# The order of the numerator's and the denominator's steps within a unit of a rational feed-forward

## The chip, the cores and the metric

One core of one Trainium2 chip runs the whole program. The core has five engines that matter here, each with its own queue of instructions executed in order: TensorE (PE, matrix products, with its weight loads listed as PEld), VectorE (DVE), ScalarE (ACT), GpSimd (POOL) and SyncE (SP), which issues most of the transfers. The metric is the device time of one execution in microseconds (us); the figure to be predicted is the median of the runs of the changed kernel.

## What is computed

Two stages follow each other. The first is a delta rule over 768 time steps for 4 batches of 8 heads, head size 48:

```python
for t in range(S):
    kt, vt, bt = (k_n[:, :, t], v[:, :, t], beta[:, :, t, None])
    y[:, :, t] = np.einsum('bhd,bhde->bhe', q[:, :, t], state)
    v_old = np.einsum('bhde,bhd->bhe', state, kt)
    state = state + bt[:, :, :, None] * np.einsum('bhd,bhe->bhde', kt, vt - v_old)
```

Its output, as 3072 tokens of 384 numbers, is the input x of the second, in which a rational function stands between two matrix products (384 to 2048 and back):

```python
h = x @ w_in
P = a[0] + a[1] * h + a[2] * h2 + a[3] * h3
Q = 1.0 + np.abs(b[0]) * np.abs(h) + np.abs(b[1]) * h2
g = P / (Q + 1e-06)
return (g @ w_out).astype(np.float32)
```

Here h2 and h3 are the square and the cube of h. The inputs and the output are 32-bit floating point, but for the two weight matrices, which arrive in 64 bit.

## The kernel before

The sequence is cut into 12 chunks of 64 steps. For each chunk an attention part (lines 489 to 722, all engines) makes the 256 tokens of the chunk, two batches on the 128 partitions and two pairs of them side by side; the state passes from chunk to chunk. `tokens` (L726 on) transposes and scales the tokens, `scalars` makes the coefficients of the rational function for the chunk. Before all this the weights are converted from 64 bit and kept in SBUF as pairs of 16-bit numbers, each product of two such pairs being three passes on PE.

The rational stage runs in units. A unit n is one chunk and one eighth of the 2048 hidden features: 256 features in two groups of 128 on the partitions, by 256 tokens, so each tile is 128 x 512. There are 96 units, and each has four steps:

- `hidden(n)`: 18 products on PE into the PSUM tile ph (two of these exist, so ph of unit n + 2 takes the place of ph of unit n).
- `numerator(n)`, the function that the change touches. ACT reads ph twice: L823 makes u = A3·h + a2 and L825 makes z = |B1·h|. DVE then reads ph three times: L826 u ← h·u, L828 w ← (z + B0)·h, L830 u ← (u + A1)·h. Between these ACT takes the absolute value of w in place (L829). u, w and z are SBUF tiles of three buffers each (tags mu, mw, mr). In some units POOL adds A0 at the end (L834).
- `quotient(n)`: ACT takes the logarithm of w + Q0 (L841) and the exponential of its negative (L842), which gives r, the reciprocal of the denominator, in the tile of z. DVE makes the upper half of g (L847, or L845 in units where POOL has added A0), then what this half has left over (L848, and L852 or POOL's L850), and POOL the lower half (L853).
- `accumulate(n)`: 12 products on PE of g with w_out into the output's accumulators, read out by ACT at L882 after the last unit of a chunk.

The program's loop interleaves them, with the attention of later chunks in between:

```python
for n in range(N + 2):
    if n < N:
        numerator(n)
    if 0 <= n - 1 < N:
        quotient(n - 1)
    attention(*divmod(n + SHIFT, NU))
    if 0 <= n - 2 < N:
        accumulate(n - 2)
    if n + 1 < N:
        hidden(n + 1)
```

This order isn't yet that of the engines' queues. The kernel is built under a planner (L1042) that puts each engine's instructions in order by the program's order, the priorities that `tc.high_priority` sets for parts of attention, and the times at which it expects operands to be ready; it also places the waits between engines. So a step of one unit can stand on an engine between two steps of another.

Of the kernel before, what the change touches and what calls it, by code (L numbers as in the profile page):

```python
# [11 lines left out]
F32 = mybir.dt.float32  # L12
BF16 = mybir.dt.bfloat16
U32 = mybir.dt.uint32
AF = mybir.ActivationFunctionType
ALU = mybir.AluOpType
# [20 lines left out]
def kernel(  # L37
# [12 lines left out]
    nc = tc.nc  # L50
# [3 lines left out]
    P = 128  # L54
# [12 lines left out]
    TG = NPAIR * P  # L67
    MB = 3
# [12 lines left out]
    sb = ctx.enter_context(tc.tile_pool(name="sb", bufs=2))  # L81
# [58 lines left out]
    for b in range(2):  # L140
        sl = slice(b * C, (b + 1) * C)
        nc.gpsimd.affine_select(
            out=mask[sl],
# [23 lines left out]
    for j in range(NB):  # L167
        nc.scalar.dma_start(
            out=bblk[j:P:NB],
# [646 lines left out]
    def numerator(n):  # L816

        c, f2 = divmod(n, NU)
        d = unit[n]
        A3, B1, A1, B0, A0, Q0 = (toks[c]["m"][:, i, f2 : f2 + 1] for i in range(6))  # L820
        ph = d.pop("ph")
        u = sb.tile([P, 2, TG], F32, tag="mu", name=f"mu{n}", bufs=MB)
        nc.scalar.activation(u, ph, AF.Identity, scale=A3, bias=a2)  # L823
        r = z = sb.tile([P, 2, TG], F32, tag="mr", name=f"mr{n}", bufs=MB)
        nc.scalar.activation(z, ph, AF.Abs, scale=B1)  # L825
        nc.vector.tensor_mul(u, ph, u)  # L826
        w = sb.tile([P, 2, TG], F32, tag="mw", name=f"mw{n}", bufs=MB)
        nc.vector.scalar_tensor_tensor(out=w, in0=z, scalar=B0, in1=ph, op0=ALU.add, op1=ALU.mult)  # L828
        nc.scalar.activation(w, w, AF.Abs)  # L829
        nc.vector.scalar_tensor_tensor(out=u, in0=u, scalar=A1, in1=ph, op0=ALU.add, op1=ALU.mult)  # L830

        by_pool = 2 <= c < NCH - 1 and f2 in (0, 4, 5, 6)
        if by_pool:
            nc.gpsimd.tensor_scalar(u, u, A0, 1.0, op0=ALU.add, op1=ALU.mult)  # L834
        d.update(u=u, w=w, r=r, A0=A0, Q0=Q0, by_pool=by_pool)
# [170 lines left out]
    for n in range(N + 2):  # L1006
        c, j = divmod(n, NU)
# [7 lines that stand above are left out]
        if n == GRP - 1 and GRP < NU:  # L1015
            tables(GRP, NU)
            scalars(0, GRP, NU)
        if n + 1 < N:
            hidden(n + 1)
# [26 lines left out]
```

## Time and profile before

| | |
|---|---|
| median of 3 runs | 858.86 us (855.03 to 863.0) |
| profiled execution, time | 857.44 us |
| its span | 855.5 us |
| DVE busy | 770.2 us (90%) |
| PE busy | 624.5 us (73%) |
| ACT busy | 593.4 us (69%) |
| POOL busy | 467.6 us (55%) |
| mean granted TensorE clock | 0.883 |

The profile is that of one execution. A row of the costliest groups names line, engine, operation, the tiles written and read, the shape and the count; then busy time in us, the mean duration of one in ns, the idle time of the engine just before these instructions, and what ended it. A row of the waits names the instruction that waited and, behind the arrow, the one that released it, with total, count and longest. A row of a timeline begins with the start from the beginning of the span and the duration, both in us; an instruction can start some 0.1 us before the end recorded for the one ahead of it on its engine. Units run from 151 us on, the last eight of them, after 810 us, without attention beside them.

### The profile page before, as it was taken

The page shows a single profiled execution, that of the slowest core. Times are in us where ns is not written, and L with a number is a line of the kernel's source. Part 1 is how long each engine was busy: PE and PEld are TensorE (multiplying, and loading weights), DVE is VectorE, ACT ScalarE, POOL GpSimd, SP SyncE. Part 2 cuts the span into 40 slices and gives each one's busy share as a digit, 9 for nine tenths or more (in the row PEclk, how much of TensorE's full clock was granted, in tenths as well). Part 3 has the DMA queues.
Part 4 walks back from the last instruction along what each step waited for, and adds up shares of the span by engine and source line. Part 5 has one row for each costly group of instructions (what it writes and reads, how often), then busy time and mean ns, then how long its engine had stood idle before and what let it go on. Part 6 is the DMA issues. An engine that isn't in the chain of part 4 may idle for free. (4 is left out here: it accounts for less than half of the span.)

```text
span 855.5 us, 23235 instructions
## 1 busy us (share of the span) xinstructions
PE 624.5 (73%) x9264; PEld 491.8 (57%) x9264; DVE 770.2 (90%) x1369; ACT 593.4 (69%) x1242; POOL 467.6 (55%) x430
## 2 busy tenths in 40 slices
PE   0230425865887697598878979888789889999885
PEld 0220424644666376476667757666677667776563
DVE  5999898899889969889899999998999998998896
ACT  4766666865666584685867777767768767887774
POOL 7665655454436345654764855746738455353622
PEclk9755555987899799889989999999989999999998
DMA  8997979966996976878879779579588572300000
GB/s 236 245 202 155 221 148 173 143 137 131 162 158 112 182 142 112 143 148 154 145 139 162 118 147 165 102 148 162 97 169 143 114 114 49 71 2 20 1 19 19
DMA packets 466508, 111.47 MB, mean 130 GB/s; under 512 B 431328, under 2 KB 463072, under 8 KB 466400
## 3 DMA queue, kind: packets, MB, share of 16 engines
q1 hardware_dynamic: 464224, 108.83, 68.5%
q8 instruction: 72, 1.18, 0.6%
q10 hardware_dynamic: 2176, 1.17, 0.4%
q14 instruction: 36, 0.29, 0.1%
HBM read 40.47 MB, written 26.23 MB: 78 GB/s over the span
## 5 line engine op out<-in xcount | busy, mean ns | idle before, releaser
L806 PE MATMUL ph<-xT,w_in 128*128 128x256 f16 x1728 | 225.6, 285 | 39.2 <-DVE mu L830 32.8
L868 PE MATMUL po<-w_out,mg 128*128 128x384 f16 x1152 | 219.0, 337 | 35.0 <-POOL mg L853 31.4
L806 PEld LDWEIGHTS <-w_in 128*128 128x128 f16 x1728 | 173.1, 102 | 76.7 <-DVE mu L830 34.9
L853 POOL TENSOR_TENSOR mg<-mu,mr 128x512 f16<-128x512 f32 x96 | 133.5, 1391 | 132.7 <-DVE mu L852 83.2
L868 PEld LDWEIGHTS <-mg 128*128 128x128 f16 x1152 | 109.3, 100 | 109.7 <-POOL mg L853 41.0
L823 ACT ACTIVATE mu<-ph,coef,msc 128x512 f32<-128x512 f32 x96 | 74.0, 771 | 49.4 <-POOL mg L853 20.2
L829 ACT ACTIVATE mw<-mw 128x512 f32<-128x512 f32 x96 | 60.4, 629 | 55.3 <-DVE mw L828 55.0
L848 DVE SCALAR_TENSOR_TENSOR mw<-mw,msc,mg 128x512 f32<-128x512 f32 x96 | 87.0, 907 | 0.7
L826 DVE TENSOR_TENSOR mu<-ph,mu 128x512 f32<-128x512 f32 x96 | 65.4, 681 | 19.4 <-ACT mr L825 14.0
L850 POOL TENSOR_TENSOR mu<-mu,mw 128x512 f32<-128x512 f32 x36 | 50.3, 1398 | 53.1 <-DVE mw L848 31.2
L403 PEld LDWEIGHTS <-kbd 128*128 128x128 f16 x1680 | 59.8, 102 | 25.5 <-issue 19.1
L828 DVE SCALAR_TENSOR_TENSOR mw<-mr,msc,ph 128x512 f32<-128x512 f32 x96 | 70.5, 735 | 0.0
L830 DVE SCALAR_TENSOR_TENSOR mu<-mu,msc,ph 128x512 f32<-128x512 f32 x96 | 70.4, 734 | 0.0
L841 ACT ACTIVATE mr<-mw,msc 128x512 f32<-128x512 f32 x96 | 69.0, 719 | 1.2
L403 PE MATMUL pu<-z,ebd 128*128 128x48 f16 x1728 | 53.7, 186 | 20.3 <-DVE z L234 14.9
L403 PEld LDWEIGHTS <-ebd 128*128 128x128 f16 x1728 | 52.8, 98 | 22.8 <-issue 21.5
L825 ACT ACTIVATE mr<-ph,msc 128x512 f32<-128x512 f32 x96 | 65.2, 679 | 0.0
L847 DVE SCALAR_TENSOR_TENSOR mg<-mu,msc,mr 128x512 f16<-128x512 f32 x60 | 59.3, 988 | 2.5 <-ACT mr L842 2.5
L842 ACT ACTIVATE mr<-mr 128x512 f32<-128x512 f32 x96 | 60.0, 625 | 1.1
L852 DVE SCALAR_TENSOR_TENSOR mu<-mu,msc,mw 128x512 f32<-128x512 f32 x60 | 55.7, 928 | 0.4
L403 PEld LDWEIGHTS <-wbd 128*128 128x128 f16 x1152 | 38.6, 101 | 28.3 <-issue 27.1
L232 POOL TENSOR_TENSOR mm<-m,mm 128x1024 f16<-128x1024 f32 x12 | 31.7, 2639 | 34.2 <-ACT mm L228 34.2
(198 smaller groups left out, 1313.7 us busy)
## 6 DMA issues: line engine op xcount, KB each, us to landing
wsi<-in_moe_w_in_dram SPq DMA_DIRECT2D x24, 256.0 KB, 5.2
xdk<-kn SPq DMA_DIRECT2D x24, 256.0 KB, 3.6
kbd<-tk SPq DMA_DIRECT2D x24, 256.0 KB, 4.5
gd<-g SPq DMA_DIRECT2D x24, 256.0 KB, 3.8
wso<-in_moe_w_out_dram SPq DMA_DIRECT2D x32, 192.0 KB, 3.8
xdq<-kn SPq DMA_DIRECT2D x24, 256.0 KB, 3.4
mbd<-mm SPq DMA_DIRECT2D x24, 256.0 KB, 5.8
wc<-img SPq DMA_DIRECT2D x24, 256.0 KB, 5.3
```

What stands on the lines that cost most here:

```text
L403: nc.tensor.matmul(dst[p][:, h], head(bd, lp, p * H + h), head(rt, rp, p * H + h), start=start and n == 0 and h == 0, stop=stop and n == l ...
L806: nc.tensor.matmul(ph[:, i], w_in[:, f2, wp, cc, i * P : (i + 1) * P], x[:, xp, cc], start=k == 0, stop=k == 3 * NCC - 1,)
L823: nc.scalar.activation(u, ph, AF.Identity, scale=A3, bias=a2)
L825: nc.scalar.activation(z, ph, AF.Abs, scale=B1)
L826: nc.vector.tensor_mul(u, ph, u)
L828: nc.vector.scalar_tensor_tensor(out=w, in0=z, scalar=B0, in1=ph, op0=ALU.add, op1=ALU.mult)
L829: nc.scalar.activation(w, w, AF.Abs)
L830: nc.vector.scalar_tensor_tensor(out=u, in0=u, scalar=A1, in1=ph, op0=ALU.add, op1=ALU.mult)
L841: nc.scalar.activation(r, w, AF.Ln, bias=Q0)
L848: nc.vector.scalar_tensor_tensor(out=w, in0=w, scalar=Q0, in1=g[:, 0], op0=ALU.add, op1=ALU.mult)
L853: nc.gpsimd.tensor_mul(g[:, 1], u, r)
L868: nc.tensor.matmul(po[p], g[:, gp, i, p * P : (p + 1) * P], w_out[:, f2, wp, i], start=f2 == lo and i == 0 and k == 0, stop=f2 == hi - 1 a ...
```

## The change

Only the order of six instructions in `numerator` is changed. Before, ACT's u and z come first, then DVE's u ← h·u, then w, |w| and the last step of u. After, ACT's z and DVE's w come first, then ACT's u, ACT's |w|, DVE's u ← h·u and the last step. No instruction is added or left out and none changes its operands or its shape. The tile of z is now asked for before that of w, and that of u last. By the line numbers after the change z is at L824, w at L826, u at L828, |w| at L829, u ← h·u at L830 and the last step at L831; all lines behind move down by one.

```diff
@@ -819,14 +819,15 @@
         d = unit[n]
         A3, B1, A1, B0, A0, Q0 = (toks[c]["m"][:, i, f2 : f2 + 1] for i in range(6))
         ph = d.pop("ph")
+
+        r = z = sb.tile([P, 2, TG], F32, tag="mr", name=f"mr{n}", bufs=MB)
+        nc.scalar.activation(z, ph, AF.Abs, scale=B1)
+        w = sb.tile([P, 2, TG], F32, tag="mw", name=f"mw{n}", bufs=MB)
+        nc.vector.scalar_tensor_tensor(out=w, in0=z, scalar=B0, in1=ph, op0=ALU.add, op1=ALU.mult)
         u = sb.tile([P, 2, TG], F32, tag="mu", name=f"mu{n}", bufs=MB)
         nc.scalar.activation(u, ph, AF.Identity, scale=A3, bias=a2)
-        r = z = sb.tile([P, 2, TG], F32, tag="mr", name=f"mr{n}", bufs=MB)
-        nc.scalar.activation(z, ph, AF.Abs, scale=B1)
+        nc.scalar.activation(w, w, AF.Abs)
         nc.vector.tensor_mul(u, ph, u)
-        w = sb.tile([P, 2, TG], F32, tag="mw", name=f"mw{n}", bufs=MB)
-        nc.vector.scalar_tensor_tensor(out=w, in0=z, scalar=B0, in1=ph, op0=ALU.add, op1=ALU.mult)
-        nc.scalar.activation(w, w, AF.Abs)
         nc.vector.scalar_tensor_tensor(out=u, in0=u, scalar=A1, in1=ph, op0=ALU.add, op1=ALU.mult)
```

## The prediction

> **What bounds the kernel now.** I read first the page's busy times, then the windows by stage, the waits, the costliest groups, and last the timelines of VectorE (DVE) and ACT around single units.
>
> ```profile
> span 855.5 us, 23235 instructions
> PE 624.5 (73%) x9264; PEld 491.8 (57%) x9264; DVE 770.2 (90%) x1369; ACT 593.4 (69%) x1242; POOL 467.6 (55%) x430
> 231.00:810.00 579.00, 489.86 (x7494) 387.50 (x7495) 529.79 (x846) 418.01 (x828) 321.39 (x259) 0.95 0.67 120
> 810.00:855.50 45.50, 33.00 (x220) 21.19 (x219) 34.63 (x50) 27.17 (x44) 11.78 (x9) 0.93 0.07 18
> ```
>
> DVE is busy for 90% of the span. The two window rows list length, PE, PEld, DVE, ACT and POOL busy: between 231 and 810 us, when units and attention run mixed, DVE is idle for 579.0 − 529.8 = 49.2 us (8.5%). No other engine is so full. So time comes or goes in two ways: DVE waits less or more, or its instructions get shorter or longer. The edit adds and removes no instruction, and all forms stay, so the 770 us of work stays but for what POOL adds to it (below). The waits are where to look.
>
> ```profile
> DVE mu L826 <- ACT mr L825: 14.0, 13, 4.2
> DVE mg L845 <- ACT mr L842: 8.0, 6, 2.1
> DVE mg L847 <- ACT mr L842: 2.5, 5, 1.0
> ACT mw L829 <- DVE mw L828: 55.0, 46, 3.3
> PE ph L806 <- DVE mu L830: 32.8, 13, 5.4
> ```
>
> Columns: total wait in us, times, longest. The first row is the largest wait of DVE and it is odd: L826 multiplies ph by u, and u comes from L823, yet it is released by L825, which writes z and nothing that L826 reads. One unit shows it in time (ACT first, then DVE; start, duration):
>
> ```profile
> 787.46 0.76 ACT L823 ACTIVATE mu<-ph,coef,msc 128x512 f32<-128x512 f32 x1
> 788.12 0.68 ACT L825 ACTIVATE mr<-ph,msc 128x512 f32<-128x512 f32 x1
> 790.27 0.63 ACT L829 ACTIVATE mw<-mw 128x512 f32<-128x512 f32 x1 [0.21 <-DVE mw L828]
> ...
> 788.90 0.69 DVE L826 TENSOR_TENSOR mu<-ph,mu 128x512 f32<-128x512 f32 x1 [1.16 <-ACT mr L825]
> 789.50 0.73 DVE L828 SCALAR_TENSOR_TENSOR mw<-mr,msc,ph 128x512 f32<-128x512 f32 x1
> 790.16 0.74 DVE L830 SCALAR_TENSOR_TENSOR mu<-mu,msc,ph 128x512 f32<-128x512 f32 x1
> 793.96 0.74 DVE L828 SCALAR_TENSOR_TENSOR mw<-mr,msc,ph 128x512 f32<-128x512 f32 x1
> 794.62 0.82 DVE L845 TENSOR_TENSOR mg<-mu,mr 128x512 f16<-128x512 f32 x1
> 795.50 0.72 DVE L830 SCALAR_TENSOR_TENSOR mu<-mu,msc,ph 128x512 f32<-128x512 f32 x1
> ```
>
> u is ready at 787.46 + 0.76 = 788.22, L825 ends at 788.80, DVE starts at 788.90. What the two share is ph: both read it from PSUM. So the reads of one ph by the two engines are kept apart, in the order of the program. Before, this costs one handoff per unit: ACT reads twice (u, z), then DVE three times (u·ph, w, u again). This is the fact on which the prediction turns.
>
> **The change, part by part.** After it the order on ph is z (ACT), w (DVE), u (ACT), u·ph and the last step (DVE): the engines alternate, with three handoffs in place of one.
>
> *The first handoff comes earlier.* DVE's first step needs one ACT read of ph, not two. Starts in a row on ACT lie 788.12 − 787.46 = 0.66 us apart, so z is ready 0.66 us sooner. Thirteen times DVE stood idle for it, so at most 13 × 0.66 = 8.6 us go. (Total wait 14.0; some waits are shorter than 0.66, so this is an upper end; the lower end is 0 where what is late next is late anyway, such as ph itself.)
>
> *r comes earlier.* w is DVE's first step and no longer waits behind L826, whose start-to-start is 789.50 − 788.90 = 0.60 us; with the 0.66 us from above w ends 1.26 us sooner after the start of the unit's ACT work. Against this u, formerly ahead of w, now stands ahead of |w| on ACT, 0.66 us. Net 0.60 us sooner for |w|, the logarithm, the exponential and so r. DVE waits for r 6 times for 8.0 us at L845 and 5 times for 2.5 us at L847: gain at most 6 × 0.60 + 2.5 = 6.1 us, and none where ACT has other work in between.
>
> *The new wait on u.* u may read ph only when w is done. In the rows: w ends at 789.50 + 0.73 = 790.23, ACT follows at 790.27 (0.04 us), u takes 0.76 us, and DVE follows ACT by 788.90 − 788.80 = 0.10 us: 0.90 us from the end of w until u·ph may start. Uncovered in every unit this would be 96 × 0.90 = 86 us. What covers it is DVE's work on the unit before or on attention: in the rows above L845 lies between L828 and L830 at 794.62, so the planner does fill there with what is ready. The trace of before has no such wait, so I bound it. Lower end 0, always filled. For the upper end I went through the DVE timeline: in 28 of 96 units the instruction right after L828 is the unit's own L830; the first and the last of these:
>
> ```profile
> 153.55 0.74 DVE L828 SCALAR_TENSOR_TENSOR mw<-mr,msc,ph 128x512 f32<-128x512 f32 x1
> 154.21 0.74 DVE L830 SCALAR_TENSOR_TENSOR mu<-mu,msc,ph 128x512 f32<-128x512 f32 x1
> ...
> 836.36 0.74 DVE L828 SCALAR_TENSOR_TENSOR mw<-mr,msc,ph 128x512 f32<-128x512 f32 x1
> 837.02 0.74 DVE L830 SCALAR_TENSOR_TENSOR mu<-mu,msc,ph 128x512 f32<-128x512 f32 x1
> ```
>
> If in those 28 nothing else was ready, the price is 28 × 0.90 = 25.2 us. The nearest row to a wait of this sort is the one on r: there too DVE needs an ACT result of the same unit after its own w, with other units to fill, and it loses 8.0 + 2.5 = 10.5 us in all. I take 10.5 us.
>
> *What queues behind u.* ACT runs in order. Where it is ahead of DVE it already stands at L829 until w is done, 46 times for 55.0 us; now it stands at u instead, at the same moment, and has one instruction more, 0.66 us, to do after it. Behind it wait other units' logarithms and exponentials and attention's casts, and through these DVE. ACT's idle time between 231 and 810 us is 579.0 − 418.0 = 161 us, three times DVE's, so I cost this at nothing beyond the 0.66 us already charged to r. Without that slack it would be up to 46 × 0.66 = 30 us on ACT.
>
> *ph is held as long as before.* Its last reader is still the last numerator step. From the start of the ACT work it was 0.66 + 0.68 + 0.10 on the way to DVE, then 0.60 + 0.66 + 0.74; now it is 0.68 + 0.10 + 0.73 + 0.90 + 0.60 + 0.74: 3.44 against 3.75 us. PE gets ph back up to 0.3 us later; 13 times that ended a wait of PE, 4 us on an engine that isn't the bound. Nothing.
>
> *Neighbours of POOL.* Some DVE instructions stretch; the columns are minimum, median and maximum in ns:
>
> ```profile
> L828 DVE SCALAR_TENSOR_TENSOR mw<-mr,msc,ph x96: 725/735/743, 153.6 to 840.5; 128x512 f32<-128x512 f32 x96
> L848 DVE SCALAR_TENSOR_TENSOR mw<-mw,msc,mg x96: 656/743/2294, 160.4 to 844.8; 128x512 f32<-128x512 f32 x96
> L847 DVE SCALAR_TENSOR_TENSOR mg<-mu,msc,mr x60: 730/746/2833, 158.5 to 844.0; 128x512 f16<-128x512 f32 x60
> L848 DVE SCALAR_TENSOR_TENSOR mw<-mw,msc,mg 128x512 f32<-128x512 f32 x96 | 87.0, 907 | 0.7
> L847 DVE SCALAR_TENSOR_TENSOR mg<-mu,msc,mr 128x512 f16<-128x512 f32 x60 | 59.3, 988 | 2.5 <-ACT mr L842 2.5
> ```
>
> L828, which reads ph, never stretches; L848 and L847, which read two SBUF tiles, go to three times their median and more. Over the medians they spend 87.0 − 96 × 0.743 = 15.7 us and 59.3 − 60 × 0.746 = 14.5 us, about 30 us. The edit moves the numerator's steps, and so shifts which quotient step lies beside which POOL instruction; the sign can't be read from before. I take 0 and keep ±6 us, a fifth of the 30. The Trainium skill ("SBUF — State Buffer", on the shared port pair) says that a DVE instruction with two SBUF inputs and a GpSimd instruction that reads SBUF shut each other out for a whole instruction; the rows agree as to which lines stretch.
>
> Sum: −8.6 − 6.1 + 10.5 = −4.2 us. The profiled execution took 857.44 us (span 855.5 and 1.9 around it); 857.4 − 4.2 = 853.2. The median of the runs is 858.86, 1.4 above the profiled one, so 854.7 us there: −0.5%.
>
> The Trainium skill ("PSUM — Partial Sum Buffer", on bank collisions) holds that ACT and DVE may not touch one PSUM bank at the same time, reads against reads included, and that software has to order them: a rule against splitting the readers of ph as this change does. L826 waiting for L825 agrees. By it the 10.5 us stand; were the reads free, u would run beside w and the sum would be −14.7 us, 844.2.
>
> **The rivals.** *Both gains, and the new wait is covered* (faster): 858.9 − 8.6 − 6.1 = 844.2. For it speaks that DVE finds filler in 68 of 96 units now, and that r arrives earlier, which makes quotient steps available just when u is awaited. Against it: both gains are upper ends, and one filler of 0.66 us doesn't cover 0.90.
>
> *The alternation becomes the bound* (slower): DVE waits for u between w and u·ph, at the units where nothing else is ready, above all at the start of each chunk and in the tail after 810 us where attention is over. At the price of 28 × 0.90 it gives 858.9 − 14.7 + 25.2 = 869.4; if the other 68 units lack 0.90 − 0.66 = 0.24 us each as well, 16 us more, 885.7. It decides from 14.7 / 0.90 = 16 uncovered units on, and passes 1% at 26. For it: ACT keeps DVE's pace only loosely, as the 46 waits at L829 show. Against: after L826, L828 and L830 DVE rarely stands still now.
>
> *The order hardly changes what waits* (no change): the planner lays out all engines anew, a filled gap opens elsewhere, since behind DVE the attention chain runs from chunk to chunk: 858.9. That the edit doesn't bite at all is unlikely, as the reads of ph follow the program.
>
> **How the numbers follow.** This kernel's runs go from 855.0 to 863.0, so under 1% can't be told from no change: faster means under 850.3, slower over 867.4. My forecast, the sum with its middle terms, and the case of no change are both "same": 0.26 and 0.12, together 0.38, own range 850 to 867. Covered and faster: 0.33. Alternation and slower: 0.29. I predict 854.7. The range takes the faster rival less the 6 us of POOL's neighbourhood, 838, and the slower one at 869.4 plus 6 and a little of its tail, 878; outside stay the far end of the alternation (0.12) and gains beyond these (0.08).
>
> **What would show it.** In the profile after, DVE's step for w should lead the unit and follow the ACT read for z; its wait should fall from 14.0 us to some 5. A new row, the step u·ph waiting for the ACT read that makes u, should stand at about 10 us; above 25 the slower rival holds. ACT should wait for w at u (near 50 us) and hardly at |w|. The waits on r should fall from 10.5 to 5 us. If the reads of ph by ACT and DVE overlap, my key fact is wrong. If DVE's idle time between the same stages stays near 49 us while the time moves, it is the instructions beside POOL that moved it.

## The result and the profile after

The changed kernel takes 851.73 us (median of 11 runs, 848.41 to 855.97) against 858.71 us for the kernel before (median of 11 runs): a ratio of 0.9915, 95% interval 0.9888 to 0.9942. It is 7.0 us faster, in the range and on the side that was forecast, where the sum said 4.2. Ratios, and the 825.58 us further down, leave out runs that fell into a slower state of the chip, over 1.5% above the kernel's fastest. The profiled execution has a span of 849.4 us, 6.1 less than before.

The page's busy times of the kernel after, and then the window that was shown of before (length, PE, PEld, DVE, ACT, POOL busy):

```profile
span 849.4 us, 23212 instructions
PE 625.6 (74%) x9264; PEld 491.3 (58%) x9264; DVE 761.0 (90%) x1369; ACT 589.5 (69%) x1242; POOL 466.9 (55%) x430
```

```profile
231.00:810.00 579.00, 491.79 (x7421) 386.04 (x7422) 528.91 (x855) 418.20 (x836) 323.08 (x260) 0.95 0.68 120
```

DVE is busy for 761.0 us and was for 770.2: 9.2 us less with the same 1369 instructions. In the window between 231 and 810 us its idle time is 50.1 us and was 49.2; that it stays there while the time moves is what the prediction named as the sign of instructions beside POOL. Over the whole span the idle time is 849.4 − 761.0 = 88.4 us and was 855.5 − 770.2 = 85.3: 3.1 us more. So by the books of this pair of profiles the time came from instructions that became shorter, not from waits.

The waits of the kernel after, to be held against the five rows of before (here and below, only rows on a unit's own steps are shown):

```profile
DVE mw L826 <- ACT mr L824: 10.6, 17, 1.2
DVE mg L848 <- ACT mr L843: 5.7, 4, 3.2
DVE mu L830 <- ACT mu L828: 4.6, 9, 1.0
DVE mg L846 <- ACT mr L843: 4.3, 5, 1.5
...
ACT mu L828 <- DVE mw L826: 54.2, 44, 3.8
...
PE ph L806 <- DVE mu L831: 33.8, 24, 5.2
```

The alternation is there: u (L828) now waits for w (L826), 44 times for 54.2 us, though it reads nothing that w writes. In no unit of the after timelines does u start before w has ended; the smallest gap of the 96 is 0.03 us. One unit, ACT first, then DVE:

```profile
785.50 0.67 ACT L824 ACTIVATE mr<-ph,msc 128x512 f32<-128x512 f32 x1
...
786.99 0.78 ACT L828 ACTIVATE mu<-ph,coef,msc 128x512 f32<-128x512 f32 x1 [0.30 <-DVE mw L826]
787.67 0.62 ACT L829 ACTIVATE mw<-mw 128x512 f32<-128x512 f32 x1
```

```profile
786.21 0.75 DVE L826 SCALAR_TENSOR_TENSOR mw<-mr,msc,ph 128x512 f32<-128x512 f32 x1 [0.30 <-ACT mr L824]
...
786.94 0.68 DVE L846 TENSOR_TENSOR mg<-mu,mr 128x512 f16<-128x512 f32 x1
787.65 0.75 DVE L849 SCALAR_TENSOR_TENSOR mw<-mw,msc,mg 128x512 f32<-128x512 f32 x1
788.32 0.68 DVE L830 TENSOR_TENSOR mu<-ph,mu 128x512 f32<-128x512 f32 x1
```

w ends at 786.96, u runs from 786.99 to 787.77, and meanwhile DVE does two quotient steps of the unit before. That is the cover of which the prediction was unsure: in 95 of the 96 units another instruction stands on DVE between w and u·ph.

The instructions that became shorter, from the groups of DVE by line; first four rows of before, then the same four after:

```profile
L848 DVE SCALAR_TENSOR_TENSOR mw<-mw,msc,mg 128x512 f32<-128x512 f32 x96 | 87.0, 907 | 0.7
L845 DVE TENSOR_TENSOR mg<-mu,mr 128x512 f16<-128x512 f32 x36 | 37.8, 1050 | 8.2 <-ACT mr L842 8.0 <-POOL mu L834 0.2
L569 DVE TENSOR_TENSOR pr<-ab,wt 128x64 f32<-128x64 f32 (+1 forms) x36 | 27.3, 786 | 0.1
L790 DVE TENSOR_TENSOR msc<-tab,sf 128x48 f32<-128x48 f32 (+1 forms) x13 | 8.6, 660 | 2.5 <-ACT sf L764 2.5
```

```profile
L849 DVE SCALAR_TENSOR_TENSOR mw<-mw,msc,mg 128x512 f32<-128x512 f32 x96 | 92.6, 965 | 0.5
L846 DVE TENSOR_TENSOR mg<-mu,mr 128x512 f16<-128x512 f32 x36 | 32.7, 908 | 5.1 <-ACT mr L843 4.3 <-POOL mu L835 0.7
L569 DVE TENSOR_TENSOR pr<-ab,wt 128x64 f32<-128x64 f32 (+1 forms) x36 | 23.8, 686 | 0.2
L790 DVE TENSOR_TENSOR msc<-tab,sf 128x48 f32<-128x48 f32 (+1 forms) x13 | 5.0, 386 | 4.2 <-ACT sf L764 4.2
```

All are DVE instructions on two SBUF tiles, and none was edited; L569 and L790 don't even belong to the unit's steps. One row rises by 5.6 us, the others fall by 5.1, 3.5 and 3.6, together 6.6 of the 9.2 us. The rest is in rows that aren't shown, some of which fall and some of which rise.

### The profile page after: what moved, and what is told of

Read it like the earlier page. It is cut to its first block, busy times and chain, and to the rows that moved or that the text cites. A ratio compares the mean times of both kernels' runs of the same rounds, so it can differ in the third digit from the quotient of the medians.

```text
span 849.4 us, 23212 instructions
## 1 busy us (share of the span) xinstructions
PE 625.6 (74%) x9264; PEld 491.3 (58%) x9264; DVE 761.0 (90%) x1369; ACT 589.5 (69%) x1242; POOL 466.9 (55%) x430
## 4 chain that ended last, share of the span: by engine, by line
DVE 41%; ACT 14%; DMA 12%; PE 11%; issue 8%; SPq 8%; POOL 3%; POOLq 0%; ACTq 0%; DVEq 0%
DVE mw L849 4%; PE ph L806 4%; PE po L869 4%; DVE w_out L327 3%; DVE mw L826 3%; DVE mg L848 3%; DVE mu L830 3%; DVE mu L831 3%; DVE mu L853 2%; ACT mu L828 2%; DVE mg L846 2%; SPq L609 2%; DVE z L234 2%; ACT mr L824 2%; ACT kp L764 2%
## 5 line engine op out<-in xcount | busy, mean ns | idle before, releaser
L806 PE MATMUL ph<-xT,w_in 128*128 128x256 f16 x1728 | 224.2, 283 | 37.1 <-DVE mu L831 33.8
L869 PE MATMUL po<-w_out,mg 128*128 128x384 f16 x1152 | 223.4, 339 | 33.5 <-POOL mg L854 27.3
L854 POOL TENSOR_TENSOR mg<-mu,mr 128x512 f16<-128x512 f32 x96 | 135.3, 1410 | 106.5 <-DVE mu L853 50.9
L828 ACT ACTIVATE mu<-ph,coef,msc 128x512 f32<-128x512 f32 x96 | 74.7, 778 | 54.4 <-DVE mw L826 54.2
L849 DVE SCALAR_TENSOR_TENSOR mw<-mw,msc,mg 128x512 f32<-128x512 f32 x96 | 92.6, 965 | 0.5
L824 ACT ACTIVATE mr<-ph,msc 128x512 f32<-128x512 f32 x96 | 64.9, 682 | 36.9 <-POOL mg L854 11.5
L826 DVE SCALAR_TENSOR_TENSOR mw<-mr,msc,ph 128x512 f32<-128x512 f32 x96 | 70.4, 737 | 10.7 <-ACT mr L824 10.6
L831 DVE SCALAR_TENSOR_TENSOR mu<-mu,msc,ph 128x512 f32<-128x512 f32 x96 | 70.8, 739 | 1.1
L830 DVE TENSOR_TENSOR mu<-ph,mu 128x512 f32<-128x512 f32 x96 | 65.2, 680 | 5.6 <-ACT mu L828 4.6
L848 DVE SCALAR_TENSOR_TENSOR mg<-mu,msc,mr 128x512 f16<-128x512 f32 x60 | 58.9, 982 | 6.2 <-ACT mr L843 5.7
L403 PEld LDWEIGHTS <-ebd 128*128 128x128 f16 x1728 | 51.7, 98 | 22.0 <-issue 20.8
L829 ACT ACTIVATE mw<-mw 128x512 f32<-128x512 f32 x96 | 60.0, 625 | 0.0
L853 DVE SCALAR_TENSOR_TENSOR mu<-mu,msc,mw 128x512 f32<-128x512 f32 x60 | 52.1, 869 | 0.2
L835 POOL TENSOR_SCALAR mu<-mu,msc 128x512 f32<-128x512 f32 x36 | 28.1, 782 | 40.5 <-DVE mu L831 28.3
L232 POOL TENSOR_TENSOR mm<-m,mm 128x1024 f16<-128x1024 f32 x12 | 31.1, 2589 | 32.7 <-ACT mm L228 30.5
```

What stands on the lines that cost most here:

```text
L403: nc.tensor.matmul(dst[p][:, h], head(bd, lp, p * H + h), head(rt, rp, p * H + h), start=start and n == 0 and h == 0, stop=stop and n == l ...
L806: nc.tensor.matmul(ph[:, i], w_in[:, f2, wp, cc, i * P : (i + 1) * P], x[:, xp, cc], start=k == 0, stop=k == 3 * NCC - 1,)
L848: nc.vector.scalar_tensor_tensor(out=g[:, 0], in0=u, scalar=A0, in1=r, op0=ALU.add, op1=ALU.mult)
L849: nc.vector.scalar_tensor_tensor(out=w, in0=w, scalar=Q0, in1=g[:, 0], op0=ALU.add, op1=ALU.mult)
L854: nc.gpsimd.tensor_mul(g[:, 1], u, r)
L869: nc.tensor.matmul(po[p], g[:, gp, i, p * P : (p + 1) * P], w_out[:, f2, wp, i], start=f2 == lo and i == 0 and k == 0, stop=f2 == hi - 1 a ...
```

## The experiments

Three theories were held against each other. A: the gain comes from the handoffs between ACT and DVE, as the prediction reckoned. B: it comes from DVE's instructions being stretched less beside POOL. C: it is the luck of the layout into which the planner fell, and another layout would have turned the sign.

**Does one profile repeat?** The kernels before and after, unchanged, profiled again.

> The kernel before, unchanged, profiled a second time, to see how far the parts of one profile repeat. First profile: span 855.5, VectorE busy 770.2 and idle 85.3 us. Theory A (the change gains by handoffs between ACT and VectorE) and theory B (it gains because VectorE's instructions stretch less beside POOL) both need the profile to repeat: VectorE busy 770 within 3 us. If busy time differs by 6 us or more between two profiles of the same kernel, the 9.2 us between before and after prove nothing.

> The kernel after, unchanged, profiled a second time. First profile: span 849.4, VectorE busy 761.0 and idle 88.4 us. Theory B: busy again 761 within 3 us and idle again no lower than before's 85. Theory A: idle below 85 in this second look, the first one being an accident.

The first fence is of before, the second of after:

```profile
span 855.4 us, 23235 instructions
PE 626.6 (73%) x9264; PEld 491.5 (57%) x9264; DVE 768.8 (90%) x1369; ACT 594.5 (70%) x1242; POOL 469.3 (55%) x430
```

```profile
span 850.9 us, 23212 instructions
PE 623.5 (73%) x9264; PEld 491.1 (58%) x9264; DVE 763.9 (90%) x1369; ACT 590.0 (69%) x1242; POOL 467.8 (55%) x430
```

Busy 768.8 (770.2 in the first profile) and 763.9 (761.0): repeated within 3 us, as B needs. Idle is 86.6 and 87.0: again not lower after. So between before and after 4.9 to 9.2 us of busy time go, and 0.4 to 3.1 us of idle time come. The rows above repeat: L845 36.7 us before and 32.7 after, L569 27.0 and 23.7, L790 7.7 and 5.0, and L848, the one that rose, 87.1 and 91.0. Not every row does: L852 fell from 55.7 to 52.1 in the first pair and rises from 54.3 to 55.4 here. Nor does the idle time between 231 and 810 us: it is 51.7 before and 46.1 after, so the sign that the prediction had named doesn't repeat. (In this window the kernel after is about one unit ahead, so it doesn't hold quite the same work.)

**POOL's product taken away.** In both kernels, the same edit; the lower half of g is left out of the result.

```diff
-        nc.gpsimd.tensor_mul(g[:, 1], u, r)
+        nc.gpsimd.memset(g[:, 1], 0.0)
```

> Before, with POOL's product for the lower half of g replaced by a plain fill with zeros of the same tile: this leaves the lower half of g out of the result, and takes away 96 POOL instructions of 1.28 us that read SBUF. Theory B: the stretched VectorE instructions (median 0.74, up to 2.8 us) shrink, VectorE busy falls by 25 to 40 us to about 735, time about 825 to 835. Theory A: POOL is no concern, time within 1% of 858.9.

> After, with the same replacement on POOL (the lower half of g is left out of the result). To be read beside the same cut of the kernel before. Theory A (handoffs): the gain stays, this is 0.6 to 1.0% faster than the other. Theory B (neighbours on POOL): the gain goes, both within 0.4% of each other. Theory C (the planner's layout happened to fall out better): anything between 1% slower and 1% faster.

Measured: 829.82 us with the order of before (ratio 0.9667, 0.9629 to 0.9706) and 825.58 with that of after (0.9632, 0.9591 to 0.9672). Busy times, before's order first:

```profile
span 828.1 us, 23116 instructions
PE 618.8 (75%) x9264; PEld 495.1 (60%) x9264; DVE 725.8 (88%) x1369; ACT 594.0 (72%) x1242; POOL 389.2 (47%) x430
```

```profile
span 823.1 us, 23062 instructions
PE 616.1 (75%) x9264; PEld 493.2 (60%) x9264; DVE 737.7 (90%) x1369; ACT 589.2 (72%) x1242; POOL 378.4 (46%) x430
```

Two things follow. POOL's 96 products cost this kernel 27.5 us of time (857.33 on the same chip against 829.82), and DVE 768.8 − 725.8 = 43 us of busy time. The time is in B's range and far outside A's; of DVE's busy time even more went than B's 25 to 40. The 27.5 us needn't all be stretching, as the fill waits for neither u nor r and their buffers come free sooner: ACT's waits for these products at L823, 16.1 us in the second profile of before, go as well. ±6 us, which I had set down for POOL's neighbourhood, was a cautious share of something large. And without them the new order gains 0.9632 / 0.9667, that is 0.4%, too near to both 0 and 0.85% for these intervals to say which. How it gains has turned round: idle falls from 102.3 to 85.4 us and busy rises by 11.9. So a gain can show as less idle time in one pair and as less busy time in another. That DVE runs into POOL more where it waits less for ACT would fit this; it isn't shown.

**The parts of the change by themselves.** First VectorE's order alone (u and z together on ACT, then w ahead of the product):

```diff
         nc.scalar.activation(u, ph, AF.Identity, scale=A3, bias=a2)
         nc.scalar.activation(z, ph, AF.Abs, scale=B1)
-        nc.vector.tensor_mul(u, ph, u)
         nc.vector.scalar_tensor_tensor(out=w, in0=z, scalar=B0, in1=ph, op0=ALU.add, op1=ALU.mult)
+        nc.vector.tensor_mul(u, ph, u)
         nc.scalar.activation(w, w, AF.Abs)
```

> One part of the change alone: ACT makes u and z together as before, and only VectorE's order is turned round, w ahead of the product of h and u. The readers of ph don't alternate, so there is no new wait on u, and the first handoff is no earlier. Theory A (handoffs): r comes 0.6 us earlier and u 0.66 us later on VectorE; the waits on r fall from 10.5 to about 5 us, the first wait stays near 14, time 850 to 855 if the earlier r is what gains, 857 to 859 if the earlier first handoff is. Theory C (layout by chance): any time from 848 to 866, with in-unit waits that don't explain it.

It takes 856.39 us, ratio 0.998 (0.9956 to 1.0004): little or nothing, between A's two figures. By its waits the first wait stays (12.6 us in 13 cases), as expected, but the waits on r don't fall to 5:

```profile
DVE mw L828 <- ACT mr L826: 12.6, 13, 2.3
DVE mg L848 <- ACT mr L843: 9.7, 8, 3.0
DVE mg L846 <- POOL mu L835: 4.0, 4, 1.7
DVE mg L846 <- ACT mr L843: 3.4, 4, 1.2
```

They are 9.7 + 3.4 = 13.1 us. r is ready earlier in the unit, 7.36 us after the unit's first ACT read of ph where it was 7.92 (means of the 96 units), yet DVE's step that uses it starts earlier by as much, after 9.03 us where it was 9.64.

Then the alternation with the numerator first:

```diff
         nc.scalar.activation(u, ph, AF.Identity, scale=A3, bias=a2)
-        nc.scalar.activation(z, ph, AF.Abs, scale=B1)
         nc.vector.tensor_mul(u, ph, u)
+        nc.scalar.activation(z, ph, AF.Abs, scale=B1)
         nc.vector.scalar_tensor_tensor(out=w, in0=z, scalar=B0, in1=ph, op0=ALU.add, op1=ALU.mult)
```

> The readers of ph alternate as after the change, but with the numerator first: u on ACT, its product on VectorE, z on ACT, w on VectorE, then the absolute value of w and the last step. Theory A: the first wait shrinks as after the change (14 to about 10 us), a wait for z of some 5 us appears in place of the wait on u, and r comes later by 0.3 us: waits on r above 10.5; time near 860, so the order of the two halves, not the alternation, makes the gain. If it is as fast as after the change (below 854), the alternation itself, that is the first handoff, is what gains.

864.47 us, ratio 1.0079 (1.0049 to 1.0108): slower than before, as A said, but by 6.8 us where A's 860 was about 1 more than before. Its waits:

```profile
DVE mw L829 <- ACT mr L827: 15.3, 15, 4.2
DVE mg L848 <- ACT mr L843: 7.5, 8, 2.0
DVE mu L825 <- ACT mu L824: 7.2, 8, 3.2
DVE mg L846 <- ACT mr L843: 3.2, 5, 1.3
```

The first wait does shrink, from 14.0 to 7.2 us, and the second one in the unit costs 15.3. r comes 9.37 us after the first ACT read, 1.45 later than before, where A said 0.3. So the alternation itself gains nothing; with the denominator second it loses.

Last, the alternation with the denominator taken to its end, |w| ahead of u (the lines are those of after):

```diff
+        nc.scalar.activation(w, w, AF.Abs)
         u = sb.tile([P, 2, TG], F32, tag="mu", name=f"mu{n}", bufs=MB)
         nc.scalar.activation(u, ph, AF.Identity, scale=A3, bias=a2)
-        nc.scalar.activation(w, w, AF.Abs)
```

> As after the change, but with the absolute value of w ahead of u on ACT. Theory A: r is 0.66 us earlier still and u as much later: waits on r fall from 10 to some 5 us, the wait on u rises from 4.6 us in 9 cases to 10 to 15 us; time 851 to 858. Theory C: any time from 848 to 866.

843.11 us, ratio 0.9837 (0.9806 to 0.9868): the fastest kernel here that makes all of g, better than both and better than either theory's figure. Busy times and waits, from an execution of 840.31 us:

```profile
span 838.6 us, 23209 instructions
PE 621.2 (74%) x9264; PEld 491.7 (59%) x9264; DVE 765.0 (91%) x1369; ACT 585.5 (70%) x1242; POOL 461.8 (55%) x430
```

```profile
DVE mu L830 <- ACT mu L829: 7.4, 13, 1.4
DVE mg L846 <- POOL mu L835: 5.2, 11, 0.8
DVE mw L826 <- ACT mr L824: 4.9, 5, 1.5
DVE mg L848 <- ACT mr L843: 1.7, 2, 1.3
DVE mg L846 <- ACT mr L843: 0.8, 2, 0.5
```

Here the waits on ACT do get shorter: those on r all but vanish (2.5 us against 10.5 before), the first wait is 4.9, and the new wait on u is 7.4, less than the 10 to 15 expected. DVE's idle time is 838.6 − 765.0 = 73.6 us, 11.7 below before, and its busy time 5.2 below. But it isn't A's way: r was to come 0.66 us earlier still, and comes 7.27 us after the first ACT read, as with the order of after (7.28). What has moved is the step that uses it, which starts later (after 9.39 us; 9.05 with the order of after).

**Two other layouts.** Two swaps in the loop over units make the planner lay out every queue anew; each was run with both orders of the numerator. In the first, accumulate stands ahead of attention; in the second, the quotient of the unit before stands ahead of the numerator.

```diff
-        attention(*divmod(n + SHIFT, NU))
         if 0 <= n - 2 < N:
             accumulate(n - 2)
+        attention(*divmod(n + SHIFT, NU))
```

```diff
-        if n < N:
-            numerator(n)
         if 0 <= n - 1 < N:
             quotient(n - 1)
+        if n < N:
+            numerator(n)
```

> Another layout of the same work: in the loop over units, accumulate(n - 2) stands ahead of attention instead of behind it; the numerator's order is that of before. It changes the planner's queues everywhere and is the partner of the next run. Alone it may come out anywhere from 845 to 875.

> The same other layout with the numerator's order of after. Theory A (the new order gains by itself): 0.5 to 1.2% faster than its partner. Theory C (the gain belongs to the one layout that the planner fell into): no steady sign, the difference within 1.5% either way, and slower as likely as faster.

> A second other layout: quotient(n - 1) stands ahead of numerator(n) in the loop; the numerator's order is that of before. Partner of the next run; alone anywhere from 845 to 875.

> The second other layout with the numerator's order of after. Theory A: 0.5 to 1.2% faster than its partner. Theory C: no steady sign.

With accumulate first: 858.42 (ratio to the kernel before 1.0004, 0.9988 to 1.0019) and 856.39 (0.9993, 0.9973 to 1.0014), a gain of 0.1% that isn't clear of nothing. With the quotient first: 859.1 (1.0011, 0.9982 to 1.004) and 850.62 (0.9905, 0.9874 to 0.9936), a gain of 1.1%. In the first of these layouts the waits on ACT within a unit, added up from the rows of first wait, u and r, fall by 5 us (26.3 to 21.1) without much of a gain; in the second they rise by 4 (16.5 to 20.4) with a gain of 8.5 us. A's 0.5 to 1.2% held in the second layout alone. DVE's busy time falls in both, by 3.5 us (772.8 to 769.3) and 8.8 (772.1 to 763.3), while its idle time stays within 2 us. So in three layouts the sign never turned, though in one of them the gain isn't clear of nothing. That speaks against C in its strict form; but the size hangs on the layout.

Was the fastest order a lucky layout as well?

> The order with the absolute value of w ahead of u on ACT (843.1 us in the first layout, 1.6% faster than before), in the other layout with accumulate ahead of attention, where the order of after came out level with before (856.4 against 858.4). If it is the earlier denominator that gains, whatever the layout: at least 0.8% faster than 858.4, under 852, with waits of VectorE on ACT inside a unit of 15 us or less. If the 843.1 was a lucky layout: 854 to 862.

845.22 us, ratio 0.9861 (0.9817 to 0.9905), against 858.42 for before's order in the same layout: 13.2 us, so the gain was not that of one layout. The other half of what was expected missed: DVE's waits on ACT within a unit are 19.7 us (7.3 first, 9.5 on u, 2.9 on r), not 15 or less. That the earlier denominator makes the gain is therefore not shown by this run.

## Why the prediction was right, and where it wasn't

The forecast was 854.7 us and "same" as the likeliest case, 0.5% down; measured are 851.73 and 0.85% down. Time and sign hold. The way there holds only in part, and that the time fell within 3 us of the forecast is in part luck: the three terms that were to make the gain came to +0.7 and −1.4 us in the two pairs of profiles, not to −4.2. In the order of its steps, with the second profile in brackets:

| step | predicted | measured |
|---|---|---|
| reads of ph alternate, u waits for w | yes | yes: 54.2 us, 44 times at u |
| first wait, 14.0 us | −8.6 at most | −3.4 (15.8 to 9.0: −6.8) |
| waits on r, 10.5 us | −6.1 at most | −0.5 (10.7 to 10.6: −0.1) |
| new wait on u | +10.5 | +4.6 (+5.5) |
| sum of the three | −4.2 | +0.7 (−1.4) |
| PE's wait for ph | about nothing | 32.8 to 33.8 us (31.2 to 31.6) |
| POOL's neighbourhood | 0, ±6 | DVE busy −9.2 (−4.9) |

- *The key fact* was right and is the surest thing here.
- *The first handoff*: mechanism right, over-sized. The waits are not fewer than before (17 for 13, and 14 for 14 in the second pair) but shorter (the longest 1.2 us for 4.2, and 1.9 for 4.2).
- *The earlier r* failed as a term. r does come earlier: over the 96 units the mean time from a unit's first ACT read of ph to the end of its exponential, taken from the timelines, is 7.92 us before and 7.28 after, the 0.6 that was worked out. But the instruction that uses r isn't fixed in its place: it starts sooner by as much (9.64 to 9.05 us), and the waits stayed.
- *The new wait* was half the size. The rival in which it becomes the bound didn't come about: 9 waits, where 16 uncovered units would have been needed. From the end of w to the start of u·ph 2.28 us pass on the mean, against the least of 0.90 that was worked out, and in most of it DVE does other work.
- *ph is held as long as before* was wrong, and cost nothing that shows. From the first ACT read of ph to the end of DVE's last one a unit takes 6.86 us and took 5.53: 1.33 longer, where 0.31 shorter was worked out. PE waits for it more often (24 times for 13, 23 for 14), but hardly longer in total.
- *u ahead of |w|* was charged 0.66 us per unit and thought to be carried by ACT's slack. In time it is the largest step tried: putting |w| first made 8.6 us more (851.73 to 843.11; 6.7 by their ratios to the kernel before as it ran beside each), more than the predicted gain of the whole change. Why isn't known, since r came no earlier by it.
- *POOL's neighbourhood* was the term mis-sized, taken at zero. In every comparison with the product in place and w first, DVE's busy time is lower than with before's order in the same layout, by 3.5 to 9.2 us, and no DVE instruction was edited. With the numerator first it isn't (770.8 us). Which rows shrink differs, though: L569 has 27.3 us before, 23.8 after and 29.1 in the fastest kernel.

Theory A alone therefore doesn't account for the 7.0 us: its three terms make nothing in the trace. Theory B has the booked time on its side, and the run without POOL's product leaves a smaller gain, but not by enough to show that B is the whole. Why two-tile instructions meet POOL less with w first was not isolated; that quotient steps now stand between numerator steps, as in the unit shown, and that POOL's instructions fall beside steps that read ph, would fit, and stays an argument.

Another thing that moved is DVE's wait for ACT in an attention step (L234 making z), from 3.2 to 9.4 us (4.4 to 7.0 in the second pair); some of the waiting may have moved there.

What the runs do show is a ranking. Mean time in a unit from the first ACT read of ph to the end of POOL's product, which is when u and z come free, beside the time of the kernel, all in the first layout:

| order | time in a unit, us | kernel, us |
|---|---|---|
| u, u·h, z, w | 17.25 | 864.47 |
| before: u, z, u·h, w | 16.71 | 858.71 |
| u, z, w, u·h | 16.29 | 856.39 |
| after: z, w, u, \|w\| | 15.58 | 851.73 |
| z, w, \|w\|, u | 15.46 | 843.11 |

The sooner the denominator's chain is under way, the shorter the unit holds its buffers and the faster the kernel, in five of five orders, though the step from the second row to the third (ratio 0.998) isn't clear of nothing. Within each of the other layouts the order is the same: 16.84, 15.64 and 15.50 us in a unit for 858.42, 856.39 and 845.22 with accumulate first, 16.84 and 15.61 for 859.1 and 850.62 with the quotient first. It is a ranking and not a proof of cause. The same 1.2 us in a unit went with 2.0 us of time in one layout and with 8.5 in the other, and the last two orders of the table differ by 0.12 us in a unit and 8.6 in time. ACT's waits for POOL to give the buffers back don't rank with it: 20.2 us before (L823), 11.5 after and 7.9 in the fastest (L824), but 14.1 in the third row and only 10.3 in the slowest kernel. The two fastest orders also ask for u's tile last, and no run took that by itself. So what makes the gain stays open.

## What to carry to other kernels

Where two engines read the same PSUM tile, look in the trace for a wait on an instruction whose result isn't used: in all 96 units after the change such readers got the tile one after the other, and their order is a thing to choose. Try first the longest chain behind that tile taken all the way, here z, w and |w|, before the shorter one gets the tile; that was the fastest in both layouts in which it ran. And when work is laid out by a planner, a wait that "goes" can be spent again elsewhere, so try the order in more than one layout before believing a gain under 1%.

## What the runs showed of the hardware

DVE's three steps that read ph from PSUM kept their duration in every unit (w: 656 to 749 ns after the change), while those with two SBUF inputs stretch, up to 2848 ns for the one at L849 with a median of 746. That longest one lay beside a product of attention on POOL:

```profile
L826 DVE SCALAR_TENSOR_TENSOR mw<-mr,msc,ph x96: 656/738/749, 150.8 to 835.0; 128x512 f32<-128x512 f32 x96
L849 DVE SCALAR_TENSOR_TENSOR mw<-mw,msc,mg x96: 653/746/2848, 159.4 to 840.4; 128x512 f32<-128x512 f32 x96
...
641.95 2.37 POOL L232 TENSOR_TENSOR mm<-m,mm 128x1024 f16<-128x1024 f32 x1 [1.01 <-ACT mm L228]
642.02 2.85 DVE L849 SCALAR_TENSOR_TENSOR mw<-mw,msc,mg 128x512 f32<-128x512 f32 x1
```

That was expected in kind; the size was not. Replacing 96 POOL products of 1.28 us with fills that read nothing took 43 us from DVE's busy time, 0.45 us for each product, and 27.5 us from the kernel. In a kernel bound by DVE this is a larger matter than any order of steps tried here.
